# Efficient attention and a channel MLP on one core: the first batches' work put in another order, and batch 0's x transposed by TensorE

## The chip, the cores and the metric

The kernel runs on one core of a Trainium2 chip. The metric is the device time in microseconds (us), and what counts is the median of the runs. Engines are named as in the profile: PE (TensorE, matmuls), DVE (VectorE), ACT (ScalarE), POOL (GpSimd), and SP (SyncE, whose queue issues nearly all DMAs).

## The reference

q, k and v have 8 batches, 8 heads, 576 tokens and 64 channels. In each head, q's exponentials are divided by their sum over the channels, k's by their sum over the tokens, and the output is `q' (k'^T v)`. The heads of one token side by side are x (8 x 576 x 512), which goes through a two-layer channel MLP with a residual:

```python
q_s = np.exp(q_s); q_s = q_s / (np.sum(q_s, axis=-1, keepdims=True) + 1e-09)
k_s = np.exp(k_s); k_s = k_s / (np.sum(k_s, axis=2, keepdims=True) + 1e-09)
kv = np.einsum('bhsd,bhse->bhde', k_s, v)
attn = np.einsum('bhsd,bhde->bhse', q_s, kv)
x = attn.transpose(0, 2, 1, 3).reshape(B, S, H * D)
xn = (x - mu) / np.sqrt(var + 1e-06) * g_ln          # mu, var over the 512 channels
out = x + np.maximum(xn @ w_ch1, 0.0) @ w_ch2         # 512 -> 2048 -> 512
```

## The kernel before

**Chunks.** Tokens are worked in 9 chunks of 512: the first 512 of each of the 8 batches, and a ninth (`xT8`, `x8`) of the 64 that are left over in each. All weights stay in SBUF in fp16.

**Attention of a batch** (`attn`, L309). q, k and v come in halves of four heads (hf 0 and 1) into staging buffers `stg` of fp32. `queries` takes exponentials on ACT (L326) and the sums, reciprocals and products on DVE (L328 to L332). `keys` and `values` are one ACT instruction each (L353 and L359, 128x1152). `eq` is transposed to `eqT`, for batch 0 by PE and copies out of PSUM (`pe_t`, L341: L349 on DVE, L350 on ACT), for all others by a DMA transpose from SP (L337). `kv` (L362) multiplies k by v; the column of ones in `vb` gives the sum of k, whose reciprocal (L378) scales `kve` (L381 on ACT, L385 on DVE). `xT` (L390) makes x transposed, `xsT`, copied out by L409 or L411; `xT_last` (L414) does the 64 tokens left over.

**Tokens** (`tokens`, L480). `xsT` is turned into x by a DMA transpose (L487, on SP), then come the statistics on DVE (L490, L491) and the inverse deviation `st` on ACT by Ln and Exp (L492, L494).

**MLP of a chunk.** The first layer, `mm1` (L521), is 16 blocks of four 128x512 matmuls (L538), each taken out of PSUM with a ReLU to `hT` (ACT L501, or DVE L503 in part of batch 0). The mean is not subtracted from x: w1 is centred once, in four column blocks (`centre_w1`, L275: a sum by a matmul with ones, L282, a copy `nm` on ACT, L284, and subtractions on DVE, L288), after it was cast and scaled by g (`load_w1`, L256: L269 on ACT, L272 on DVE). For batch 0, `mm1_open` (L509) starts blocks 0 to 3 with the first heads alone. The second layer of batch 0 is `mm2` (L672): 64 plain matmuls in 16 groups of four (L681), evicted by L694 once the statistics are there. From batch 1 on it is `mm2_split` (L591), seven products of half size with sums of `hT` (`S`, L554) and of w2 (`T`, `w2_sums`, L560); partial results are read out between products by `add_x` into `cp` and by `final` into `ot` (all L628).

**PSUM.** Eight banks: four `pg` for the MLP, four `pa` for the attention and for w1's sums; batch 1's first four mm1 blocks also use `pa`. `zeros` (L705) are matmuls of zeros that fill PE's waits in the head.

**Order.** Each step is added to a `Plan` (L22) with an engine, an estimated duration, what it reads and writes, and a class `cls`; `after` adds an order without data. `Plan.order` simulates the engines and a DMA queue, and at each moment takes the ready step of the lowest class. The instructions are then written out in that order, and each engine executes its own strictly in that order. So a class or an estimate changes nothing but places in the engines' queues. Fills are as many as the planner's gap holds (L119). In the head, `first_w1` (L717) puts block 0's centring and `mm1_open` between the transposes and the k and v of batch 0's second heads.

Of the kernel before, what the change touches and what calls it, by code (L numbers as in the profile page):

```python
# [21 lines left out]
class Plan:  # L22
# [33 lines left out]
    def order(self):  # L56
# [11 lines left out]
        queue = 1.2  # L68
# [5 lines left out]
        while done < n:  # L74
            best = None
            for eng, lst in pend.items():
                if not lst:
                    continue
                f = free.get(eng, 0.0)
                t0 = max(f, min(ready[i] for i in lst))  # L80
                c = min((i for i in lst if ready[i] <= t0 + 1e-9), key=lambda i: T[i][4])
                if best is None or t0 < best[0]:
                    best = (t0, c, eng)
            t0, i, eng = best
            pend[eng].remove(i)
            _, dur, fn, deps, _, land, mb = T[i][:7]
            start[i] = t0
            issued = end = t0 + dur
            if mb or land:
                queue = max(queue, t0 + min(dur, 0.6)) + mb / 0.385  # L90
                issued = max(end, queue - (9.0 if dur < 2.0 else 0.8))
                end = max(queue, issued) + land
            free[eng] = issued
            for u in users[i]:
                hop = (self.HOP if T[u][0] != eng or mb or land else 0.0) + T[u][9]
                ready[u] = max(ready[u], issued if i in T[u][7] else end + hop)
                left[u] -= 1
                if left[u] == 0:
                    pend.setdefault(T[u][0], []).append(u)
            seq.append(i)  # L100
            done += 1
# [9 lines left out]
    def emit(self):  # L111
        seq = self.order()
        open_, at = None, 0.0
        for i in seq:
            if self.tasks[i][0] == "PE":
# [3 lines left out]
                n = int((self.start[i] - at - 0.1) / self.FILL)  # L119
# [20 lines left out]
def kernel(  # L140
# [46 lines left out]
    hold = sb([P, 1], FP32, "hold")  # L187
# [50 lines left out]
    def load(dst, src, w, mb):  # L238
        gate[1] = plan.add("SP", 0.55, lambda: nc.sync.dma_start(dst, src), w=w, mb=mb, land=2.0,
                           after=tuple(gate[0]) + ((gate[1],) if gate[1] is not None else ()))  # L240
# [15 lines left out]
    def load_w1(blk):  # L256
        after = state["kve"] if blk == 1 else state["ev"][1] if blk == 2 else ()
        cls = 0.5 if blk else 0
        for kp in range(2):
            s = nxt("stg", NST)  # L260
            load(stg[s][:, :1024].rearrange("p (a n) -> p a n", a=2),
                 w1_src[:, 2 * kp : 2 * kp + 2, blk * 512 : blk * 512 + 512], sk(s), 0.524 if blk else 0.65)
            for a in range(2):
                ko = 2 * kp + a
                dst = w1_sb[:, ko, blk * 512 : blk * 512 + 512]
                src = stg[s][:, a * 512 : a * 512 + 512]
                gk = g_sb[:, ko : ko + 1]
                if ko % 2:
# [6 lines left out]
    def centre_w1(blk):  # L275

        gi = nxt("pa", 4)
        cs = slice(blk * 512, blk * 512 + 512)
        wk = [("w1", blk, ko) for ko in range(KO1)]
        def f():  # L280
            for ko in range(KO1):
                nc.tensor.matmul(pa[gi], ones, w1_sb[:, ko, cs], start=(ko == 0), stop=(ko == KO1 - 1))  # L282
        plan.add("PE", 0.216 * KO1, f, r=wk + ["ones"], w=[("pa", gi)], cls=0)
        plan.add("ACT", act_t(512), lambda: nc.scalar.copy(nm, pa[gi]), r=[("pa", gi)], w=["nm"], cls=0)  # L284
        for k0, k1, m0, m1 in ([(0, 2, 0, 4), (2, 4, 0, 4)] if blk == 0 else [(0, 4, 0, 1), (0, 4, 1, 4)]):
            n = (m1 - m0) * P
            c0 = blk * 512 + m0 * P
            plan.add("DVE", dve_t((k1 - k0) * n, 2), lambda k0=k0, k1=k1, c0=c0, n=n, m0=m0: nc.vector.tensor_tensor(  # L288
                w1_sb[:, k0:k1, c0 : c0 + n], w1_sb[:, k0:k1, c0 : c0 + n],
                nm[:, m0 * P : m0 * P + n].unsqueeze(1).to_broadcast([P, k1 - k0, n]), op=ALU.subtract),  # L290
                r=["nm"] + wk, w=[("w1c", 4 * blk + m, k) for m in range(m0, m1) for k in range(k0 // 2, k1 // 2)], cls=0)

# [10 lines left out]
    ident_b = sb([P, P], BF16, "ident_b")  # L303
    plan.add("POOL", 1.5, lambda: make_identity(nc, ident_b), w=["ident"])
    XK = lambda u: [("xsT", u, j, g) for j in range(J) for g in range(G)]
# [3 lines left out]
    def attn(b, kind, between=None, exps=(), sums_=(), kvs=()):  # L309
# [31 lines left out]
        def pe_t(hf):  # L341
# [5 lines left out]
            plan.add("PE", 0.7, f, r=[("eq", u, hf), "ident"], w=[("pa", t) for t in tb], cls=0)  # L347
            dst = eqT[u][:, JT * hf : JT * hf + 8]
            plan.add("DVE", dve_t(1024, 2), lambda: nc.vector.tensor_copy(dst, v16[0]), r=[("pa", tb[0])], w=[("eqT", u, hf)], cls=0)  # L349
# [7 lines left out]
        def values(hf, s):  # L357
            vd, va = vb[u][:, hf].rearrange("p j s d -> p s j d")[:, :, :, :D], sv(s)
            plan.add("ACT", act_t(QW), lambda: nc.scalar.copy(vd, va), r=sk(s), w=[("vb", u, hf, i) for i in range(2)],  # L359
                     cls=cls, slack=late, after=tuple(exps) + (tuple(state["ev"][-1][-1:]) if steady else ()))  # L360

        def kv(hs):  # L362
# [9 lines left out]
            ids = []  # L372
            plan.add("PE", 0.1 + 0.42 * len(hs), f, r=[("ek", u, h) for h in hs] + [("vb", u, h, i) for h in hs for i in range(2)],
                     w=[("pa", a) for x in ab for a in x], cls=0, slack=SLACK if steady else 0.2, after=kvs)
            for n, h in enumerate(hs):
                for e in range(2):
                    a, g = ab[n][e], 2 * h + e
                    plan.add("DVE", 0.17, lambda a=a, g=g: nc.vector.reciprocal(rz[:, g : g + 1], pa[a][:, D : D + 1]),  # L378
                             r=[("pa", a)], w=[("rz", g)], cls=0.35 if steady else 0)
                    if e and not steady:  # L380
# [3 lines left out]
                    else:  # L384
                        ids.append(plan.add("DVE", 0.28, lambda a=a, g=g: nc.vector.tensor_scalar_mul(  # L385
                            kve[u][:, g, :], in0=pa[a][:, :D], scalar1=rz[:, g : g + 1]),
                            r=[("pa", a), ("rz", g)], w=[("kve", u, g)], cls=0.35 if steady else 0))
            return ids

        def xT(hs, after=()):  # L390
# [12 lines left out]
            for n, h in enumerate(hs):  # L403
                for i in range(2):
# [3 lines left out]
                    if kind == "first" and i == 1:  # L408
# [23 lines left out]
        if kind == "first":  # L432
            lq, lk, lv = [load_half(b, t, 0, x) for t, x in ((q, 0), (k, 0), (v, 0.25))]
# [5 lines left out]
            pe_t(0)  # L439
# [3 lines left out]
            pe_t(1)  # L443
            between()
            lk, lv = [load_half(b, t, 1) for t in (k, v)]
# [3 lines left out]
            state["kve"] = kv([1])  # L449
            xT([1])  # L450
# [13 lines left out]
        else:  # L464
            gate[1] = dma_t()
            state["eqT"] = gate[1], tokens(0, 0.7, (gate[1],))
# [13 lines left out]
    def tokens(c, cls=1, after=(), stats=()):  # L480
# [4 lines left out]
        else:  # L485
            src, r = xT8, [("xT8", b, i) for b in range(B) for i in range(2)]
        i = plan.add("SP", 2.2, lambda: nc.sync.dma_start_transpose(x.rearrange("p j (k c) -> p (j k) c", k=KO1), src.rearrange("p n t -> p (n t)")),  # L487
                 r=r, w=[(xk, j) for j in range(J)], mb=0.9, land=0.6, after=after)
        for j in range(J):
            plan.add("DVE", dve_t(512), lambda j=j: nc.vector.bn_stats(bst[:, j, :], x[:, j, :]), r=[(xk, j)], w=[("bst", j)], cls=cls, slack=2.0 if c else 0.5, after=stats)  # L490
# [4 lines left out]
                 r=[(stk, "v", j) for j in range(J)], w=[(stk, "r", j) for j in range(J)], cls=0)  # L495
# [64 lines left out]
    def w2_sums(k0, n, after):  # L560
# [6 lines left out]
        def tt(i, a, b, r):  # L567
            eng, e = ("POOL", nc.gpsimd) if i == 2 else ("DVE", nc.vector)
            plan.add(eng, 1.2 if i == 2 else dve_t(256 * n, 2), lambda: e.tensor_tensor(T[i][:, ks], a, b, op=ALU.subtract),  # L569
                     r=r + (["hold"] if i == 2 else []), w=tk(i), cls=2, after=after if i == 2 else ())  # L570
# [101 lines left out]
    def mm2(c):  # L672
# [4 lines left out]
        for k0 in range(0, KO2, 4):  # L677
            for j in range(J):
# [5 lines left out]
                if j == 0:  # L684
                    ids.append(i)
                if (k0, j) in steps:
                    second_x(steps.index((k0, j)), (i,))
        plan.fill(ids[0], ids[-1], zeros(pg[gis[0]], False))
        evs = []
        for hf in range(2):  # L690
            o = nxt("ot", NOT)
            for i in range(2):
                j = 2 * hf + i
                ev = plan.add("DVE", dve_t(512), lambda o=o, i=i, j=j: nc.vector.scalar_tensor_tensor(  # L694
# [3 lines left out]
                evs.append(ev)  # L698
            store(c, o, hf)
        return evs[:1]  # L700
# [16 lines left out]
    def first_w1():  # L717
        centre_w1(0)
# [21 lines left out]
    for b in range(B):  # L740
        if b:
            state["tok"] = tokens(b, 0.7, stats=state["stats"])
        if b == B - 1:
            tokens(8, 0.7, stats=state["stats"])
        ids = mm1(b, b > 0, () if b else opened)
# [5 lines left out]
        before = (ids[-1], state["rstd"])  # L751
        if b == 0:
            evs = mm2(b)
            plan.add("POOL", 0.2, lambda: nc.gpsimd.tensor_copy(hold, ot[0][:, 0, :1]), r=[("ot", 0, 0)], w=["hold"])
            for k0 in range(0, HK, 2):
                w2_sums(k0, 2, evs)
        else:
            mm2_split(b)
    mm1(8, True)
# [37 lines left out]
```

The softmax here doesn't subtract the row's maximum and nothing guards it: scores larger than these inputs give would overflow.

## Time and profile before

| | |
|---|---|
| median of 9 runs | 280.9 us (280.61 to 281.1) |
| the profiled execution | 281.06 us |
| its span | 279.3 us |
| PE busy | 270.1 us, 97% |
| DVE busy | 199.2 us, 71% |
| ACT busy | 168.2 us, 60% |
| POOL busy | 5.9 us, 2% |
| TensorE's granted clock | 0.998 |
| DMA | 55.35 MB, about 387 GB/s from 10 to 40 us |

The span is what the profiler covers of the execution; the rest of its time lies outside. In the profile's timeline a row is start, length, engine, line, operation, `out<-in` and, in brackets, the engine's idle time before the row and what ended it. In the chain of waits a row is start, length and what the time went to, followed back from the last instruction. A matmul of 512 columns is listed with 0.38 us, but in a stream they start 0.216 us apart.

### The profile page before, as it was taken

Reading aid. Unit: us, or ns where it says so; the run is one execution under the profiler, and the core shown is the slowest. Engines: PE = TensorE matmul, PEld = TensorE weight load, DVE = VectorE, ACT = ScalarE, POOL = GpSimd, SP = SyncE. Lnnn points to the kernel's source line nnn. Section 1 sums busy time; section 2 is a strip of 40 time slices with the busy share of each in tenths; the row PEclk is TensorE's granted clock in tenths of the full one; section 3 lists DMA queues with packets and bytes.
Section 4 is the critical chain, followed back from the end, with each engine's and each line's share of the span. In section 5 each row is a group of like instructions: output and inputs, shape, how many; then the busy total and the mean of one; then the engine's idle time right before and its main releaser. Section 6 shows DMA issues by size and latency. Waiting matters only on the chain.

```text
span 279.3 us, 5657 instructions
## 1 busy us (share of the span) xinstructions
PE 270.1 (97%) x2327; PEld 164.5 (59%) x2327; DVE 199.2 (71%) x406; ACT 168.2 (60%) x273; POOL 5.9 (2%) x15
## 2 busy tenths in 40 slices
PE   8989999989799999999999999999999999999994
PEld 3434444435674478447844784478447844874583
DVE  2867897499859967976599569865995773641572
ACT  4768985499478595568566946685665077016500
POOL 1000000060000000000000000000000000000000
PEclk9999999999999999999999999999999999999999
DMA  7999998999987894579858985697544350023004
GB/s 257 354 386 387 387 389 196 270 341 236 318 266 153 207 392 73 150 153 387 131 151 109 396 166 150 137 392 143 153 84 78 75 153 0 0 51 101 0 2 151
DMA packets 57953, 55.35 MB, mean 198 GB/s; under 512 B 36676, under 2 KB 37192, under 8 KB 57928
## 3 DMA queue, kind: packets, MB, share of 16 engines
q1 hardware_dynamic: 57776, 54.86, 68.1%
q8 instruction: 18, 0.29, 0.4%
q10 hardware_dynamic: 152, 0.13, 0.1%
q14 instruction: 7, 0.06, 0.1%
HBM read 36.70 MB, written 9.44 MB: 165 GB/s over the span
## 4 chain that ended last, share of the span: by engine, by line
PE 78%; DVE 13%; DMA 6%; ACT 1%; issue 1%; SPq 0%
PE pg L538 38%; PE pg L618 32%; DMA stg<-in_moe_w_ch_dram 4%; PE pg L705 3%; DVE zq L328 2%; DVE eq L332 2%; DMA x<-xsT 2%; DVE S L554 2%; DVE bst L490 2%; PE pa L370 1%; PE pa L618 1%; PE pa L398 1%; DVE ot L694 1%; DVE T L569 1%; PE pa L282 1%
## 5 line engine op out<-in xcount | busy, mean ns | idle before, releaser
L501 ACT ACTIVATE hT<-pg 128x512 f16<-128x512 f32 x134 | 78.9, 600 | 67.2 <-PE pg L538 66.6
L538 PE MATMUL pg<-xsT,w_sb 128*128 128x512 f16 x488 | 108.2, 379 | 1.0 <-ACT hT L501 0.4
L538 PEld LDWEIGHTS <-w_sb 128*128 128x128 f16 x568 | 54.9, 98 | 65.9 <-issue 1.3
L618 PEld LDWEIGHTS <-S 128*128 128x128 f16 x512 | 49.7, 98 | 7.6 <-issue 1.5
L618 PE MATMUL pg<-T,S 128*128 128x256 f16 x368 | 42.2, 273 | 1.5 <-DVE cp L628 1.5
L618 PEld LDWEIGHTS <-hT 128*128 128x128 f16 x384 | 37.0, 98 | 8.2 <-issue 3.0
L554 DVE TENSOR_TENSOR S<-hT 128x1024 f16<-128x1024 f16 x32 | 21.8, 685 | 23.7 <-ACT hT L501 23.7
L628 DVE SCALAR_TENSOR_TENSOR cp<-pg,st,x 128x256 f32<-128x256 f32 x46 | 20.2, 478 | 13.3 <-PE pg L618 12.6
L618 PE MATMUL pg<-w_sb,hT 128*128 128x256 f16 x248 | 29.4, 273 | 0.0
L490 DVE BATCH_NORM_STATS2 bst<-x 128x6 f32<-128x512 f16 x36 | 24.1, 671 | 7.1 <-DMA x<-xsT 7.1
L628 DVE SCALAR_TENSOR_TENSOR ot<-pg,st,cp 128x256 f32<-128x256 f32 x47 | 20.5, 477 | 11.6 <-PE pg L618 11.5
L332 DVE TENSOR_TENSOR eq<-eq,rzq 128x1152 bf16<-128x1152 bf16 x16 | 22.7, 1418 | 0.5
L359 ACT CAST vb<-stg 128x1152 f16<-128x1152 f32 x16 | 18.7, 1168 | 5.5 <-DMA stg<-in_v_dram 5.4
L328 DVE TENSOR_REDUCE zq<-eq 128x18 f32<-128x1152 bf16 x16 | 21.5, 1345 | 0.3 <-ACT eq L326 0.3
L326 ACT ACTIVATE eq<-stg 128x1152 bf16<-128x1152 f32 x16 | 18.8, 1177 | 2.9 <-DMA stg<-in_q_dram 2.7
L353 ACT ACTIVATE ek<-stg 128x1152 bf16<-128x1152 f32 x16 | 18.7, 1166 | 2.6 <-DMA stg<-in_k_dram 2.6
L411 ACT CAST xsT<-pa 128x512 f16<-128x512 f32 x30 | 15.5, 598 | 2.4 <-PE pa L398 2.4
L705 PE MATMUL pg<-zero 128*128 128x512 f16 x52 | 14.3, 422 | 1.2 <-DVE zero L224 1.2
L618 PE MATMUL pg<-w_sb,S 128*128 128x256 f16 x128 | 15.3, 273 | 0.0
L618 PE MATMUL pg<-T,hT 128*128 128x256 f16 x120 | 14.4, 272 | 0.4 <-DVE ot L628 0.4
L681 PE MATMUL pg<-w_sb,hT 128*128 128x512 f16 x64 | 14.7, 380 | 0.0
L538 PE MATMUL pg<-xT,w_sb 128*128 128x512 f16 x64 | 14.0, 379 | 0.0
(64 smaller groups left out, 164.6 us busy)
## 6 DMA issues: line engine op xcount, KB each, us to landing
stg<-in_q_dram SPq DMA_DIRECT2D x16, 576.0 KB, 5.6
stg<-in_k_dram SPq DMA_DIRECT2D x16, 576.0 KB, 7.3
stg<-in_v_dram SPq DMA_DIRECT2D x16, 576.0 KB, 8.0
out_dram<-ot SPq DMA_DIRECT2D x33, 256.0 KB, 3.6
stg<-in_moe_w_ch_dram SPq DMA_DIRECT2D x16, 512.0 KB, 10.1
out_dram<-ot SPq DMA_DIRECT2D x1, 512.0 KB, 2.8
x<-xsT SPq DMA_TRANSPOSE x8, 6.7
out_dram<-ot SPq DMA_DIRECT2D x1, 128.0 KB, 2.7
```

Source lines behind the costliest of these rows:

```text
L326: plan.add("ACT", act_t(QW), lambda: nc.scalar.activation(e.rearrange("p j (s d) -> p s j d", s=2), sv(s), AF.Exp), r=sk(s), w=[("eq", u, ...
L328: plan.add("DVE", dve_t(QW), lambda: nc.vector.reduce_sum(zq[:, hf], eh, axis=AX.X), r=[("eq", u, hf)], w=[("zq", hf)], cls=qcls, after=sums_)
L332: plan.add("DVE", dve_t(QW), lambda: nc.vector.tensor_tensor(eh, eh, rzq[:, hf].to_broadcast([P, 2 * JT, D]), op=ALU.mult), r=[("rzq", hf) ...
L353: plan.add("ACT", act_t(QW), lambda: nc.scalar.activation(ek[u][:, hf].rearrange("p j (s d) -> p s j d", s=2), sv(s), AF.Exp), r=sk(s), w= ...
L359: plan.add("ACT", act_t(QW), lambda: nc.scalar.copy(vd, va), r=sk(s), w=[("vb", u, hf, i) for i in range(2)], cls=cls, slack=late, after=t ...
L490: plan.add("DVE", dve_t(512), lambda j=j: nc.vector.bn_stats(bst[:, j, :], x[:, j, :]), r=[(xk, j)], w=[("bst", j)], cls=cls, slack=2.0 if ...
L501: nc.scalar.activation(hT[:, m, :], bank, AF.Relu)
L538: nc.tensor.matmul(bank[gi], w1_sb[:, ko, m * P : m * P + P], xt[:, ko], start=(ko == 0), stop=(ko == KO1 - 1))
L554: plan.add("DVE", dve_t(256 * n, 2), lambda: nc.vector.tensor_tensor(S[i][:, ks], a, b, op=op), r=r, w=sk(i), cls=0.3 if k0 else 0.45)
L618: nc.tensor.matmul(g[i][0], fa(k, i), fb(k), start=(first and k == 0 and (i == 0 or g[0][1] != g[1][1])), stop=(last and k == HK - 1), ski ...
L628: nc.vector.scalar_tensor_tensor(dst[:, i, :], in0=g[i][0], scalar=sti[:, 4, 2 * t0 + i : 2 * t0 + i + 1], in1=src[:, i, :], op0=ALU.mult, ...
L705: nc.tensor.matmul(bank_, zero[:, :P], zero, start=start, stop=start, skip_group_check=True)
```

## The change

All of it lies in what happens up to batch 2; batch 0 changes most.

1. The v cast of batch 0's second heads is two instructions: channel group 0 on DVE, 1 on ACT.
2. `centre_w1(0)` uses the bank `pg[opened[2]]`; its second subtraction is held back behind the kv of the second heads, and the copies of the second transposes (`pe_t_evac`) behind the first subtraction. The `nm` copies get a lower class.
3. w1's casts are split otherwise over ACT and DVE (`on_act`), and those of block 2 on ACT need only follow the `nm` copy before them.
4. Batch 0's x is made by 16 PE transposes into two `pa` banks and two DVE copies, inside `mm2`, with no DMA transpose.
5. `w2_sums` is all on DVE; the POOL instructions and `hold` are gone.
6. In `kv` the two reciprocals come ahead of the two products; which engine scales `kve` and in which class is set by batch. `xT` of batch 0 has three ACT copies and one DVE copy.
7. The planner's constants: DMA queue start, rate, landing time, the margin taken off a fill, the class of batch 1's statistics.

```diff
-        queue = 1.2
+        queue = 2.4
...
-                n = int((self.start[i] - at - 0.1) / self.FILL)
+                n = int((self.start[i] - at - 0.45) / self.FILL)
...
-    hold = sb([P, 1], FP32, "hold")
...
-        gate[1] = plan.add("SP", 0.55, lambda: nc.sync.dma_start(dst, src), w=w, mb=mb, land=2.0,
+        gate[1] = plan.add("SP", 0.55, lambda: nc.sync.dma_start(dst, src), w=w, mb=mb, land=0.65,
...
+        on_act = ((1,), (0, 1, 3), (1,), (1, 3))[blk]
...
+                after = state["kve"] if blk == 1 and (kp or ko not in on_act) else ()
+                if blk == 2:
+                    after = (state["nm"],) if ko in on_act else state["ev"][1]
...
-                if ko % 2:
+                if ko in on_act:
...
-        gi = nxt("pa", 4)
+        if blk:
+            gi = nxt("pa", 4)
+            bank, bk = pa[gi], ("pa", gi)
+        else:
+            bank, bk = pg[opened[2]], ("pg", opened[2])
...
-        plan.add("ACT", act_t(512), lambda: nc.scalar.copy(nm, pa[gi]), r=[("pa", gi)], w=["nm"], cls=0)
+        state["nm"] = plan.add("ACT", act_t(512), lambda: nc.scalar.copy(nm, bank), r=[bk], w=["nm"], cls=-0.5)
...
+        if blk == 0:
+            state["sub"] = sub(0, 2, 0, 4)
+            return lambda: sub(2, 4, 0, 4)
+        sub(0, 4, 0, 1)
+        sub(0, 4, 1, 4)
...
+    ident_h = sb([P, P], FP16, "ident_h")
+    plan.add("POOL", 1.5, lambda: make_identity(nc, ident_h), w=["ident_h"])
...
+            if kind == "first" and hf == 1:
+                plan.add("DVE", dve_t(QW // 2, 2), lambda: nc.vector.tensor_copy(vd[:, 0], va[:, 0]), r=sk(s), w=[("vb", u, hf, 0)], cls=cls)
+                plan.add("ACT", act_t(QW // 2), lambda: nc.scalar.copy(vd[:, 1], va[:, 1]), r=sk(s), w=[("vb", u, hf, 1)], cls=cls)
+                return
...
+            kcls = 0 if not steady else 0.35 if b > 2 else -0.6
...
-                    if e and not steady:
+                for e in range(2):
+                    a, g = ab[n][e], 2 * h + e
+                    if e and (b == 1 or b == 2 or h and not b):
...
-                    if kind == "first" and i == 1:
+                    if kind == "first" and i == 1 and h == 1:
...
-            lq, lk, lv = [load_half(b, t, 0, x) for t, x in ((q, 0), (k, 0), (v, 0.25))]
+            lq, lk, lv = [load_half(b, t, 0, x) for t, x in ((q, 0), (k, 0), (v, 0))]
...
-            pe_t(0)
+            pe_t_evac(0, *pe_t(0))
...
-            pe_t(1)
+            t1 = pe_t(1)
             between()
+            pe_t_evac(1, *t1, (state["sub"],))
...
             state["kve"] = kv([1])
+            state["sub2"]()
             xT([1])
...
-            state["eqT"] = gate[1], tokens(0, 0.7, (gate[1],))
+            state["eqT"] = (gate[1],)
...
+        i = None
+        for hf in range(2) if c == 0 else ():
+            t = nxt("pa", 4)
+            v = pa[t].bitcast(FP16)
+            def f(hf=hf, v=v):
+                for n in range(8):
+                    nc.tensor.transpose(v[:, n * P : n * P + P], src[:, 8 * hf + n, :], ident_h)
+            plan.add("PE", 0.52, f, r=r + ["ident_h"], w=[("pa", t)], cls=0, after=after)
+            plan.add("DVE", dve_t(1024, 2), lambda hf=hf, v=v: nc.vector.tensor_copy(
+                x[:, 2 * hf : 2 * hf + 2, :], v.rearrange("p (j n) -> p j n", j=2)), r=[("pa", t)], w=[(xk, 2 * hf), (xk, 2 * hf + 1)], cls=cls)
+        if c:
+            i = plan.add("SP", 2.2, lambda: nc.sync.dma_start_transpose(x.rearrange("p j (k c) -> p (j k) c", k=KO1), src.rearrange("p n t -> p (n t)")),
+                     r=r, w=[(xk, j) for j in range(J)], mb=0.9, land=0.6, after=after)
...
-            eng, e = ("POOL", nc.gpsimd) if i == 2 else ("DVE", nc.vector)
...
+            plan.add("DVE", dve_t(256 * n, 2), lambda: nc.vector.tensor_tensor(T[i][:, ks], a, b, op=ALU.subtract),
+                     r=r, w=tk(i), cls=2)
...
+                if (k0, j) == (4, 2):
+                    tokens(0, 0.7, (i,))
...
-            state["tok"] = tokens(b, 0.7, stats=state["stats"])
+            state["tok"] = tokens(b, 0.7 if b > 1 else 0.35, stats=state["stats"])
...
-            plan.add("POOL", 0.2, lambda: nc.gpsimd.tensor_copy(hold, ot[0][:, 0, :1]), r=[("ot", 0, 0)], w=["hold"])
```

## The prediction

> **What bounds the kernel now.** I read the 40 slices first (is TensorE full everywhere?), then the chain of waits in order of time (where does it leave TensorE?), then TensorE's own timeline of the head. The slices:
>
> ```profile
> PE   8989999989799999999999999999999999999994
> ```
>
> Each is 7 us; the holes are in the first eleven. The chain's later part is TensorE alone:
>
> ```profile
> 102.94 8.84 PE pg L618 x80
> 111.78 9.50 PE pg L538 x44
> 121.28 0.76 PE pa L370 x72
> 122.04 4.42 PE pg L538 x20
> ```
>
> Columns: start, length, what. Each begins where the last ends, so from about 83.8 us a batch costs its matmuls, and no step of the change takes one away there. The head is different:
>
> ```profile
> 24.34 0.43 DVE w_sb L288
> ...
> 45.95 5.95 DMA x<-xsT
> 51.91 0.02 issue
> 51.93 0.70 DVE bst L490
> ...
> 55.83 2.73 DVE ot L694 x4
> ...
> 74.43 0.89 DVE cp L628 x2
> 75.31 0.04 issue
> 75.36 5.41 PE pg L618 x48
> ```
>
> The path runs from a weight that is centred late, over the DMA transpose of x0, its statistics and batch 0's eviction, to batch 1's first `cp`. What TensorE loses there, in brackets (idle before, and who ended it):
>
> ```profile
> 18.55 0.48 PE L370 MATMUL pa<-vb,ek 64*64 64x65 f16 x36 [0.92 <-ACT vb L359]
> 24.82 1.90 PE L538 MATMUL pg<-xsT,w_sb 128*128 128x512 f16 x8 [0.30 <-DVE w_sb L288]
> 56.63 3.61 PE L538 MATMUL pg<-xsT,w_sb 128*128 128x512 f16 x16 [0.29 <-DVE ot L694]
> 60.67 7.07 PE L538 MATMUL pg<-xsT,w_sb 128*128 128x512 f16 x32 [0.43 <-ACT hT L501]
> 75.36 1.91 PE L618 MATMUL pg<-T,S 128*128 128x256 f16 x16 [1.50 <-DVE cp L628]
> 81.72 1.91 PE L618 MATMUL pg<-T,hT 128*128 128x256 f16 x16 [0.41 <-DVE ot L628]
> ```
>
> By starts the loss is a little larger, since listed ends overlap: batch 1's 64 mm1 matmuls take 52.72 to 67.57 = 14.85, the same 64 at 223.22 take 13.81, so 1.04 is lost; batch 1's mm2 takes 67.57 to 83.82 = 16.25 against 13.18 (98.60 to 111.78) + 0.76 for the kv matmuls inside it = 13.94, so 2.31 is lost. One 4-matmul block is 0.865.
>
> **v cast on two engines.** v of the second heads lands at 17.34 (ACT starts its 1.17 cast then, kv follows at 18.55). Half on ACT: 0.60 for a 128x512 cast, so 0.65 for 576. Half on DVE: 0.68 for a 1024 fp32 cast (L298), so about 0.5; at the slow rate of L409 (0.69 for 512) 0.75. I take 0.65: kv at 18.05, 0.5 earlier (0.4 to 0.5). On DVE the first centring subtract (0.63), the eqT copy (0.6), two reciprocals and a product (0.5) now queue behind the v half, so behind 17.34. The subtract ends at 18.45, kv at 18.5: no new wait. `mm1_open` runs 18.55 to 20.3, xT follows at 20.4 (ACT's two weight casts of 0.65 and kve end at 20.15).
>
> **Centring ahead of copies.** Before, block 1's subtract stood on DVE behind a cast of block 3, landing 23.92. Now the last cast ahead of it is block 2's, landing 22.56 (the second of DVE's two at 21.97 + 1.10 - 0.48): cast to 23.05, subtract of the first quarter 0.43, 23.5. TensorE: xT 20.4, centring at 20.9 once ACT and DVE have cast block 1's last pair, 0.86, xT_last 0.18, 8 matmuls 1.73: 23.75. So block 4 starts at 23.75 instead of 24.82, **1.07 earlier**, the v gain and the two 0.22 fills counted. The casts that changed engine fit between evictions; I find blocks 5 to 15 back to back, mm2 of batch 0 at 35.87. Block 0's centring sum goes to bank pg2, copied out by 16.1, opened by mm1 at 19.4: no wait.
>
> **x0 by TensorE.** 16 transposes. L346 does 9 in 0.63 on the chain, 0.07 each: 1.12. The Trainium skill ("TensorE: Matmul & The Clock Gate", Part 4) gives about 275 ns for one in a kernel's context[...]; that would be 4.4 and would turn the whole change to a loss of about 1.1. I take the row: same shape, two-byte data, back to back, and nothing waits on one alone. In before the DMA transpose left SP 1.84 and landed 5.95 after its issue, and DVE sat 3.81 idle for it. Timeline now: mm2 group 11 ends 45.4; kv needs v casts (44.82 and 46.35; the loads of k and v land 1.5 apart, the load queue is the limit, so these stay); kv, one group, kv: 47.2; transposes to 48.4; four groups and three small products: mm1 of batch 1 at **52.65**, against 52.72. The head's 1.07 is eaten by the transposes; the gain has to come from behind.
> DVE: kv's reciprocals and products to 47.85, two copies out of PSUM at 0.61 (L349) to 49.1, four statistics pairs at 0.79 to 52.3, Ln and Exp 0.55 on ACT: 52.85. Eviction of batch 0 52.9 to 55.6 instead of 55.83 to 58.56. Bank pg0 is wanted at 56.1: the stalls of 0.29 and 0.43 go, **1.04** by starts.
>
> **T2 from POOL to DVE, hold removed.** Four at 0.385 = 1.54 on DVE, at 42 to 48, where before had 0.32 + 0.69 + 3.81 idle; costs nothing while w2's cast for k0=8 still ends (41.4) before 42.8. POOL makes one more identity (0.2 + 0.29) ahead of `ident_g`, which TensorE wants at 5.7: hidden. The POOL group goes, and with it the one `eq` product that took 2.35 beside it where the others take 1.36.
>
> **x1's statistics earlier.** SP's queue without x0: eqT of batch 1, two q loads, x1's transpose at 51.85 (ACT's last xsT copy), landing about 57.2 (4.3 to 6.0 for these). DVE then: eviction 55.6, sum 56.9, reciprocal 57.2, x1's four pairs 60.5, eq product 61.9, sum, reciprocal, product 64.8, S sums; `cp` of 11*11 at 69.6. TensorE, leaving mm1 at 66.5, wants it at 70.0: the 1.50 goes. With no wait at all mm2 would end at 66.5 + 13.94 = 80.45: 3.37 won.
>
> **What is late next.** ACT's order. Two kve scalings of batch 2 move to ACT and stand behind batch 3's two q exponentials. Those wait for loads that SP issues after eqT of batch 2 (its DVE product ends 64.8, SP takes 3.2: 68.05). In before the issues at 68.88 and 69.4 landed at 74.74 and 76.22; so 73.9 and 75.4 to 75.5. ACT: 75.5 + 1.16 + 0.31 = 77.0. TensorE arrives at xT at 76.1: **0.9 lost**. Then two k exponentials (landing 78.4 at the latest) to 79.55, four xsT copies 2.05: 81.6, and TensorE is at 81.35: 0.3 lost. Batch 2 starts at 81.65 instead of 83.82: **-2.15**. After that the orders on PE, DVE and ACT differ only in which bank or which reciprocal comes first; ten microseconds lie between xsT and its use: 0.
> Planner constants, the 0.45 margin for fills: no instruction's price, only order and fewer fills (52 to 33 zero matmuls), all in waits: 0, but see the clock.
>
> **Sum.** The profiled execution took 281.06, 1.76 of it outside its span of 279.3; 281.06 - 2.15 = 278.9. It stood 0.16 above the median of 280.9, so 278.75; I say **278.8**.
>
> **Rivals.**
> (1) *No wait on ACT's q.* If the loads land by 74 (eqT moves a little faster) nothing is late: 280.9 - 3.4 = 277.5. For it: nothing else is due. Against: landing hangs on 4.6 to 6.5 us of DMA transpose ahead. 20%.
> (2) *TensorE's clock falls.* Fills go from 27 to 22 ahead of the first transposes and to none from about 14 us on. I count idle of 1.2, 0.35, 0.65 and 1.5 between 11 and 18.1; the longest in before was 0.92. The skill, same page ("HAM oscillation" and its table of rules), warns of idle gaps above some 3 us; a gap of 1.5 is inside that. But it also says that transposes do not count as work, and then 15.3 to 18.1 is one gap of 2.8. Price from the trace: cold loads stand 0.427 apart up to 4.6 us, warm 0.216; 3.4 us cold lose 1.7. As kv of batch 1 slips with it, so does all behind: 278.8 + 1.7 = 280.5, no change. I take the gap rule; before's 0.92 and its granted clock of 0.998 say no more. 13%.
> (3) *Slower: eqT of batch 1 runs into v.* Its `eq` product ends at 40.8 instead of 42.66, so SP issues this transpose while k, v0 and v1 are still under way; in before only v0 and v1 were. If transfers share instead of queueing, v1 lands up to one transpose (4.6) late, at 49.8; kv of batch 1 then starts at 51.0, not 46.75, and copies, statistics, eviction, x1 and q slide by 4.2: 283. It decides from v1 landing after 47.7 (2.15 late). Against: in before k0, k1, v0, v1 came at an even 1.5 although the transpose was issued between. Small delays give 279 to 280. 11%.
> (4) *The change is not what it says*, since a planner sets the order: no; built, DVE, ACT, PE and SP stand in the order used above.
>
> **Numbers.** Likeliest case 56%, its own range 278.1 to 279.6. With (1), 20%; (2), 13%; (3), 11%. The range 277.2 to 280.7 takes in the no-wait bound and the cold clock, and leaves out (3). A difference under 0.2% (0.56 us) cannot be told from none: below 280.3 counts as faster (56 + 20 and a little of the rest, 0.77), to 281.5 as the same (0.12), above as slower (0.11).
>
> **What would show it.** Right: kv of batch 0's second heads about 18.05; mm1 block 4 at 23.7; 16 transposes in about 1.2; mm1 of batch 1 near 52.6 with no gap; `cp` not waited for; an idle piece near 76 before L398's counterpart, ended by ACT's kve behind q; batch 2 at 81.6. Wrong: matmuls 0.427 apart after 18; v1's cast after 47.7; x1 landing after 58; any gap inside a batch past 84, which I put at nothing and which would count six times.

## The result, and the profile after

The changed kernel takes **277.72 us** (median of 10 runs, 277.37 to 278.22), the one before 280.79 in the runs beside it (31 runs, 280.41 to 281.66): ratio 0.989, 95% interval 0.9882 to 0.9898. The profiled execution took 277.66, its span 275.9, at a granted clock of 1.000. PE is busy for 268.3 us, DVE 199.0, ACT 168.1, POOL 1.7 (5.9 before).

The chain of waits of the changed kernel (start, length, what), up to batch 2:

```profile
9.04 11.97 DMA stg<-in_moe_w_ch_dram
...
21.04 0.72 ACT w_sb L271
21.76 1.47 ACT hT L538 x3
...
23.27 1.91 PE pg L575 x8
...
52.46 3.45 PE pa L575 x16
55.91 10.36 PE pg L575 x48
66.27 5.24 PE pg L654 x48
```

Before, the chain ran from batch 0 over the DMA transpose of x0, its statistics, batch 0's eviction and `cp`. Now it is the load of w1 up to 21.04, then ACT, and from 23.27 on nothing but TensorE to the last instructions. At 23.27 two things had just ended: the three ReLUs on ACT that the chain names (23.23), and the first piece of block 1's subtraction on DVE (22.79 + 0.42 = 23.21). It was the subtraction that block 4 waited for: in a run below block 4 starts at 22.46, while the same three ReLUs end at 23.33. TensorE's own timeline (start, length, engine, line, operation, and in brackets the idle time before it):

```profile
16.40 0.48 PE L391 MATMUL pa<-vb,ek 64*64 64x65 f16 x36
...
23.27 1.91 PE L575 MATMUL pg<-xsT,w_sb 128*128 128x512 f16 x8 [1.03 <-ACT hT L538]
...
35.37 9.66 PE L717 MATMUL pg<-w_sb,hT 128*128 128x512 f16 x44
...
46.75 1.07 PE L519 MATMUL pa<-ident_h,xsT 128*128 128x128 f16 x16
47.66 1.03 PE L717 MATMUL pg<-w_sb,hT 128*128 128x512 f16 x4
...
52.30 3.62 PE L575 MATMUL pa<-xsT,w_sb 128*128 128x512 f16 x16
55.75 10.52 PE L575 MATMUL pg<-xsT,w_sb 128*128 128x512 f16 x48
66.11 3.66 PE L654 MATMUL pg<-w_sb,hT 128*128 128x256 f16 x32
69.60 1.91 PE L654 MATMUL pg<-T,S 128*128 128x256 f16 x16
...
75.80 0.63 PE L422 MATMUL pa<-eqT,kve 64*64 64x512 bf16 x8
```

From 16.40 to the end the timeline lists a single wait on TensorE, the one at block 4 (23.27). The 64 matmuls of batch 1's mm1 take 66.11 - 52.30 = 13.81, what they take undisturbed. Where the time came from, by starts on TensorE:

| stage begins | before | predicted | after |
|---|---|---|---|
| mm1 block 4, batch 0 | 24.82 | 23.75 | 23.27 |
| mm2, batch 0 | 36.92 | 35.87 | 35.37 |
| mm1, batch 1 | 52.72 | 52.65 | 52.30 |
| mm2, batch 1 | 67.57 | 66.5 | 66.11 |
| mm1, batch 2 | 83.75 | 81.65 | 80.21 |
| mm1 of the ninth chunk | 249.10 | | 245.80 |

So 1.55 is won by mm2 of batch 0. At mm1 of batch 1 0.42 of it is left: the transposes take 0.91, and small pieces the rest. Then 1.04 comes from mm1's stalls, since batch 0's eviction starts at 52.50 instead of 55.83, and 2.08 from mm2's: 3.54 in all.

```profile
52.50 2.73 DVE L731 SCALAR_TENSOR_TENSOR ot<-pg,st,x 128x512 f32<-128x512 f32 x4 [0.29 <-ACT st L531]
```

Batch 2 gives back 0.24 (by the chain it takes 28.20, before 27.96: 0.13 more in its first 44 matmuls, 0.11 more in the kv matmuls behind them), and 3.30 reaches the end in this pair of executions. The medians differ by 3.07.

At the place where the prediction saw the next wait, SP's timeline (the DMA transpose of batch 2's `eq`, then batch 3's q) and ACT's:

```profile
64.29 3.18 SPq L351 DMA_TRANSPOSE eqT<-eq  x1
67.51 1.10 SPq L238 DMA_DIRECT2D stg<-in_q_dram  x2
```

```profile
71.92 1.16 ACT L340 ACTIVATE eq<-stg 128x1152 bf16<-128x1152 f32 x1 [1.84 <-DMA stg<-in_q_dram]
72.99 0.30 ACT L405 ACTIVATE kve<-pa,rz 128x64 f16<-128x64 f32 x1
73.45 1.16 ACT L340 ACTIVATE eq<-stg 128x1152 bf16<-128x1152 f32 x1 [0.16 <-DMA stg<-in_q_dram]
74.52 0.30 ACT L405 ACTIVATE kve<-pa,rz 128x64 f16<-128x64 f32 x1
```

Both `kve` scalings do stand behind batch 3's q exponentials, but the second ends at 74.82, ahead of xT at 75.80.

### The profile page after: what moved, and what is told of

The parts are those of the page before. It is cut to its first block, busy times and chain, and to the rows that moved or that the text cites. A ratio compares the mean times of both kernels' runs of the same rounds, so it can differ in the third digit from the quotient of the medians.

```text
span 275.9 us, 5670 instructions
## 1 busy us (share of the span) xinstructions
PE 268.3 (97%) x2324; PEld 163.9 (59%) x2324; DVE 199.0 (72%) x412; ACT 168.1 (61%) x274; POOL 1.7 (1%) x12
## 4 chain that ended last, share of the span: by engine, by line
PE 90%; DMA 7%; ACT 1%; SPq 0%; DVE 0%; issue 0%
PE pg L575 43%; PE pg L654 35%; PE pg L717 5%; DMA stg<-in_moe_w_ch_dram 4%; DMA stg<-in_v_dram 2%; PE pa L391 2%; PE pa L422 1%; PE pa L654 1%; PE pa L575 1%; PE pa L288 1%; ACT hT L538 1%; PE pa L445 0%; ACT vb L380 0%; PE pa L519 0%; SPq L238 0%; ACT w_sb L271 0%
## 5 line engine op out<-in xcount | busy, mean ns | idle before, releaser
L346 DVE TENSOR_TENSOR eq<-eq,rzq 128x1152 bf16<-128x1152 bf16 x16 | 21.6, 1353 | 0.3
L380 ACT CAST vb<-stg 128x1152 f16<-128x1152 f32 x15 | 17.6, 1172 | 2.9 <-DMA stg<-in_v_dram 2.9
L740 PE MATMUL pg<-zero 128*128 128x512 f16 x33 | 10.7, 486 | 1.2 <-DVE zero L223 1.2
```

The source lines that it names most:

```text
L346: plan.add("DVE", dve_t(QW), lambda: nc.vector.tensor_tensor(eh, eh, rzq[:, hf].to_broadcast([P, 2 * JT, D]), op=ALU.mult), r=[("rzq", hf) ...
```

## The experiments

Times are compared with runs of the kernel before on the same chip. "Alone" means one part of the change put into the kernel before; "undone" means one part taken out of the changed kernel. Where a run is set against the changed kernel, two medians are subtracted that were not taken side by side; worked out from the ratios instead, the differences are 0.65 for x0, 0.84 for the statistics, 0.67 for the zeros and 1.7 for the first subtraction. Two of the undone parts (x0 and the statistics) and x0 alone went through the planner, which also moved other steps (in the first two, batch 2's `kve` scalings on ACT), so their times are those of the part with its new order.

**The kernel before, once more.** No edit.

> The kernel before once more, for its trace. In the first trace v of batch 0's second heads landed at 17.3 us, after the change at 15.6 or earlier, although SP issued it at 4.6 in both. If landing is set by the order of casts and issues, v lands again at 17.0 to 17.6 here and batch 3's q some 9.1 us after the issue of batch 2's eqT transpose. If it scatters from execution to execution, v lands anywhere from 15 to 17.5, with the time near 280.8 all the same, because block 4 of mm1 still waits for w1's third block (24.8).

281.6 in one run, span 279.8. The landing scatters. v of the second heads was there by 15.85 in this execution (17.34 in the first trace), kv ran at 17.68, and still block 4 waited 0.97 and started at 24.62. DVE's timeline says why:

```profile
22.39 0.49 DVE L272 TENSOR_SCALAR w_sb<-stg,g_sb 128x512 f16<-128x512 f32 x1 [0.82 <-DMA stg<-in_moe_w_ch_dram]
23.74 0.49 DVE L272 TENSOR_SCALAR w_sb<-stg,g_sb 128x512 f16<-128x512 f32 x1 [0.87 <-DMA stg<-in_moe_w_ch_dram]
24.15 1.28 DVE L288 TENSOR_TENSOR w_sb<-w_sb,cp 128x512 f16<-128x512 f16 x2
```

Two casts that wait for their load stand ahead of the subtraction (L288) that block 4 needs. In the same view of the changed kernel the last such cast ahead of it is the one for the load before, and the subtraction comes 1.36 earlier:

```profile
21.04 0.49 DVE L274 TENSOR_SCALAR w_sb<-stg,g_sb 128x512 f16<-128x512 f32 x1 [0.94 <-DMA stg<-in_moe_w_ch_dram]
22.39 0.48 DVE L274 TENSOR_SCALAR w_sb<-stg,g_sb 128x512 f16<-128x512 f32 x1 [0.87 <-DMA stg<-in_moe_w_ch_dram]
22.79 1.29 DVE L294 TENSOR_TENSOR w_sb<-w_sb,cp 128x512 f16<-128x512 f16 x2
```

So the head's gain is the place of this subtraction in DVE's queue, counted in loads of w1 that land about 1.35 apart. It does not hang on one execution: with the head of before (four profiles: the two of this kernel, x0 alone, the statistics alone) block 4 starts at 24.37 to 24.82 and mm2 of batch 0 at 36.48 to 36.92; with the changed head (the changed kernel, x0 undone, the statistics undone) at 23.00 to 23.40 and 35.10 to 35.51. The old place of the subtraction was not put back alone.

**v cast whole on ACT, undone through the planner.**

```diff
-            if kind == "first" and hf == 1:
+            if False:
```

> The kernel after, with the second heads' v cast whole by ACT. Theory (block 4 of mm1 waits for the landing of w1's third block at 22.4, so that nothing won before counts): 277.7 within 0.3. Rival (the prediction's own count, v gives 0.4 to 0.5 of the head's gain): 278.1 to 278.3.

282.23 (6 runs), ratio 1.0054 (1.0037 to 1.0071): slower than before. It is no test of the cast. Block 4 started at 23.39, 0.12 later; but the planner, told of a longer cast, set everything behind in another order: kv of batch 1's second heads at 50.52 (46.34 in the changed kernel), mm1 of batch 1 at 54.85 and of batch 2 at 85.76, with eight waits on the way. One estimate in the plan was worth 4.5 us; neither expectation had that. The next run keeps the order.

**v cast whole on ACT, every place kept.** The DVE step stays in the plan and does nothing; ACT casts both groups.

```diff
-                plan.add("DVE", dve_t(QW // 2, 2), lambda: nc.vector.tensor_copy(vd[:, 0], va[:, 0]), r=sk(s), w=[("vb", u, hf, 0)], cls=cls)
-                plan.add("ACT", act_t(QW // 2), lambda: nc.scalar.copy(vd[:, 1], va[:, 1]), r=sk(s), w=[("vb", u, hf, 1)], cls=cls)
+                plan.add("DVE", dve_t(QW // 2, 2), lambda: None, r=sk(s), w=[("vb", u, hf, 0)], cls=cls)
+                plan.add("ACT", act_t(QW // 2), lambda: nc.scalar.copy(vd, va), r=sk(s), w=[("vb", u, hf, 1)], cls=cls)
```

> The changed kernel with one thing undone: v of batch 0's second heads is cast whole on ACT (1.17 us instead of 0.65 beside DVE), and every instruction's place in every queue is kept. My prediction gave the cast 0.4 to 0.5 us at kv. Theory (T): what limits the head is the landing of w1 behind v, so block 4 of mm1 stays within 0.15 of 23.27 although kv of the second heads comes 0.4 later, and the time is 277.7 to 278.0. Rival (R): kv's 0.5 goes through to block 4 and from there to the end, 278.2 to 278.3.

277.71 (5 runs), ratio 0.9886 (0.9867 to 0.9905): no different from the changed kernel. kv waited 0.56 for ACT, but block 4 still hung on the subtraction (22.62 here), and mm2 of batch 0 started at 35.19. The split cast is worth nothing here.

**x0 by DMA transpose, undone.**

```diff
-            state["eqT"] = (gate[1],)
+            state["eqT"] = gate[1], tokens(0, 0.7, (gate[1],))
...
-        for hf in range(2) if c == 0 else ():
+        for hf in ():
...
-        if c:
+        if True:
...
-                if (k0, j) == (4, 2):
-                    tokens(0, 0.7, (i,))
```

> The kernel after, with batch 0's x made by a DMA transpose behind eqT of batch 1 again, and no PE transposes. Theory (their 0.9 us on TensorE buys an eviction 2 to 3 us earlier): x0 lands near 51, eviction from 54.8, TensorE waits for pg banks again, eqT of batch 2 leaves about 2 us later and with it q and k of batch 3: 280.0 us (279.2 to 280.8). Rival (the DMA transpose was hidden, the transposes only cost): 276.8, 0.9 below the kernel after.

278.29 (4 runs), ratio 0.9913 (0.9898 to 0.9928): 0.57 more than the changed kernel, far less than expected, and barely clear of noise (the two intervals meet at 0.9898). TensorE, without the transposes, begins mm1 of batch 1 at 51.43 and meets no wait in it, because x0's statistics start at 49.85 (51.93 before). Of these 2.08, 0.80 come from the issue of the transpose (45.15 on SP, 45.95 before) and 1.28 from its landing, 4.7 after the issue instead of 5.95; why it landed sooner, no run shows. Against the changed kernel they are 1.23 late, and so is the rest of DVE's queue behind them: batch 0's eviction at 53.74 instead of 52.50, eqT of batch 2 on SP at 65.58 instead of 64.29, and q of batch 3 lands later. ACT's timeline, then TensorE's:

```profile
73.23 1.16 ACT L340 ACTIVATE eq<-stg 128x1152 bf16<-128x1152 f32 x1 [3.72 <-DMA stg<-in_q_dram]
74.30 0.50 ACT L405 ACTIVATE kve<-pa,rz 128x64 f16<-128x64 f32 x2
```

```profile
74.29 0.98 PE L422 MATMUL pa<-eqT,kve 64*64 64x512 bf16 x8
...
78.43 0.25 PE L445 MATMUL pa<-eqT,kve 64*64 64x64 bf16 x6 [0.27 <-ACT xsT L435]
```

xT stands at 74.29 and is drawn out to 0.98 (0.63 in the changed kernel): it waits for `kve`, which ACT runs from 74.30, behind q. That is the wait of the prediction, in another kernel.

**x0 by PE transposes, alone.** The core of the edit to the kernel before, with the identity, the two DVE copies and `tokens(0)` inside `mm2` as in the change:

```diff
+            plan.add("PE", 0.52, f, r=r + ["ident_h"], w=[("pa", t)], cls=0, after=after)
...
+                if (k0, j) == (4, 2):
+                    tokens(0, 0.7, (i,))
```

> The kernel before with one part of the change alone: batch 0's x by 16 PE transposes and two DVE copies in place of the DMA transpose. Theory (T): the three stalls behind batch 0's eviction (0.29, 0.43) and the 1.50 at cp get smaller, since eviction comes some 3 us earlier and SP's queue is one transpose shorter, while the transposes cost 0.9 on TensorE: net gain 1.5 to 2.0, 278.8 to 279.3. Rival (R): without the other parts x1's statistics stay late behind batch 0's eviction or the DVE sums, the 1.50 stays, and the 0.9 of the transposes is only just repaid by the mm1 stalls: 280.4 to 280.9.

279.86 (4 runs), ratio 0.9959 (0.9945 to 0.9974), between the two expectations. All four stalls between 52 and 84 are gone, the 1.50 at `cp` among them, though x1's statistics are still late here (the last pair at 67.79). So mm1 of batch 2 begins at 81.29, 2.46 earlier than before. At the end 1.88 of that is left (the last DVE instruction at 273.50 against 275.38); in the profiled run the last store then took 3.2 us to land, where the others took 2.2 or 2.3, so that the span is only 1.0 shorter. The median is 1.24 below that of before; whether the store was as late in the other runs, no profile shows. T2 stays on POOL here (53.70 to 58.19), and DVE's first `eq` product, which runs beside it, is slow again:

```profile
57.07 2.35 DVE L334 TENSOR_TENSOR eq<-eq,rzq 128x1152 bf16<-128x1152 bf16 x1
...
61.01 1.36 DVE L334 TENSOR_TENSOR eq<-eq,rzq 128x1152 bf16<-128x1152 bf16 x1
```

**Batch 1's statistics late, undone.**

```diff
-            state["tok"] = tokens(b, 0.7 if b > 1 else 0.35, stats=state["stats"])
+            state["tok"] = tokens(b, 0.7, stats=state["stats"])
```

> The kernel after, with batch 1's statistics put back into class 0.7, so that they stand behind the q products and the first S sums on DVE. Theory (the gain is made behind 52 us, by x1's statistics coming before the sums): the last statistics pair ends near 70, cp near 71.4, TensorE waits 1.5 to 2 us for it, 279.5 us (279.0 to 279.9). Rival (batch 0's earlier eviction alone pays; x1's statistics would be in time anywhere): 277.5 to 278.0.

278.53 (4 runs), ratio 0.992 (0.9905 to 0.9935): 0.81 more than the changed kernel, between the two expectations. x1's last pair comes at 69.20 on DVE (59.06 in the changed kernel), and a wait for `cp` is back on TensorE, two thirds of the one before. DVE's timeline, then TensorE's:

```profile
73.90 1.66 DVE L664 SCALAR_TENSOR_TENSOR cp<-pg,st,x 128x256 f32<-128x256 f32 x4 [0.75 <-PE pg L654]
```

```profile
74.83 1.91 PE L654 MATMUL pg<-T,S 128*128 128x256 f16 x16 [0.97 <-DVE cp L664]
```

This `cp` had itself waited 0.75 for one of TensorE's products, not for the statistics (the first `cp` ran at 70.70). So the wait came with the order that the planner made for late statistics; that the statistics alone cause it is not shown.

**Batch 1's statistics early, alone.** The same line, put into the kernel before.

> The kernel before with one part alone: the class of batch 1's statistics (x1's four pairs come ahead of the sums of eq on DVE). Theory (T): x0's eviction still ends at 58.6 there, so x1's pairs end about 62 and delay eq's product and SP's transpose of eqT behind it; the 1.50 at cp shrinks, but q and k of batch 3 land some 3 us later: net 279.6 to 280.3. Rival (R): the 1.50 goes whole and nothing is late, 279.3 or less; or the delay at q takes it all, 280.6 and more.

280.89 (10 runs), ratio 0.9996 (0.9982 to 1.0009): nothing. x1's pairs now run from 59.48 to 62.7 on DVE, but batch 0's eviction still ends at 58.3, and the second `eq` product comes 1.8 us later behind them (65.90 instead of 64.09), with the sums S after that. TensorE's waits have moved, not gone:

```profile
71.83 1.91 PE L618 MATMUL pg<-T,S 128*128 128x256 f16 x16 [0.40 <-DVE cp L628]
...
81.04 0.60 PE L618 MATMUL pg<-T,hT 128*128 128x256 f16 x4 [0.96 <-DVE ot L628]
```

T2 ran on POOL from 56.53 to 61.03 in this run; the first `eq` product came behind it, at 62.95, and took 1.36. So it is the time beside POOL that made this product slow, 2.35, in the runs where they met. The edit pays only once x0 comes early. Parts of one change are not to be added up.

**No zeros after 8 us.**

```diff
-                n = int((self.start[i] - at - 0.45) / self.FILL)
+                n = int((self.start[i] - at - 0.45) / self.FILL) if self.start[i] < 8.0 else 0
```

> The changed kernel without any matmul of zeros after 8 us (the ones before stay). Theory (T): the clock does not fall, since idle pieces of about 1 us left it at 1.0 in the changed kernel; the matmuls from 17 to 24 us start 0.216 apart, and the time is 277.7 within 0.3. Rival (R): the fills from 8 to 15 us hold the clock up; without them matmuls after 15 us start 0.427 apart for some 3 us, block 4 of mm1 comes 1 to 1.7 later, and the time is 278.7 to 279.5.

17 of the 33 zero matmuls go. 278.82 (4 runs), ratio 0.9914 (0.9894 to 0.9935): 1.1 more by the medians, where the intervals still touch; the trace shows that the rival was right. Busy time in three stretches (core time, then PE with its instructions, PEld, DVE, ACT and POOL, the granted clock, the share of DMA and GB/s):

```profile
8.00:11.00 3.00, 1.18 (x46) 0.99 (x46) 2.12 (x6) 2.49 (x3) 0.00 (x0) 1.00 1.02 327
11.50:21.00 9.50, 8.20 (x64) 3.11 (x64) 7.17 (x15) 6.00 (x11) 0.00 (x0) 0.50 1.05 392
22.00:26.00 4.00, 4.00 (x26) 1.73 (x25) 3.85 (x9) 3.53 (x7) 0.00 (x0) 1.00 1.05 388
```

With TensorE busy for 1.18 of the 3 us before 11, the clock is granted at half from 11.4 to 21.6, and mm2 of batch 0 begins at 36.37 instead of 35.37. In the changed kernel the same 3 us are full with zeros (3.00), and the clock stays at 1.00.

**The first subtraction ahead of block 2's casts.**

```diff
-                    after = (state["nm"],) if ko in on_act else state["ev"][1]
+                    after = (state["nm"],) if ko in on_act else (state["sub1"],)
...
-        sub(0, 4, 0, 1)
+        state["sub1"] = sub(0, 4, 0, 1)
```

> The changed kernel with one dependence moved: the subtraction of block 1's first quarter of w1 is put on DVE ahead of block 2's casts there, which waited for w1 to land (0.94 and 0.87 us of DVE idle) and held the subtraction back. Theory (T): block 4 of mm1 then starts when the centring sum is copied out, at 22.1 to 22.4 instead of 23.27; about 0.9 of it reaches batch 1, and the time is 276.7 to 277.0. Rival (R): blocks 8 to 11 now wait for their later casts, or kv of batch 1 for v (cast at 45.08, kv not before 46.3), and the gain is lost by mm1 of batch 1: 277.5 to 277.8.

279.63 (4 runs), ratio 0.995 (0.9936 to 0.9964): slower than the changed kernel by 1.9, which neither expectation had. Block 4 came without a wait at 22.46. But the planner now put a w2 cast ahead of block 2's subtraction, and that cast waits for its load. DVE, then TensorE:

```profile
29.07 0.69 DVE L310 CAST w_sb<-stg 128x1024 f16<-128x1024 f32 x1 [1.09 <-DMA stg<-in_moe_w_ch_dram]
29.68 0.42 DVE L605 TENSOR_TENSOR T<-w_sb 128x512 f16<-128x512 f16 x1
30.01 1.28 DVE L294 TENSOR_TENSOR w_sb<-w_sb,cp 128x512 f16<-128x512 f16 x2
```

```profile
25.92 1.89 PE L288 MATMUL pa<-w_sb,ones 128*128 128x512 f16 x8
30.49 7.09 PE L575 MATMUL pg<-xsT,w_sb 128*128 128x512 f16 x32 [2.67 <-DVE w_sb L294]
```

It is the same fault one block later, and dearer.

**Places moved by hand.** In these the planner's order stands, and a list moves single steps within their engine's queue (each to just behind another; only the list is shown):

```diff
...
+    (('cast2', 0), ('sub1', 1)),
+    (('cast2', 1), ('cast2', 0)),
+    (('cast2', 2), ('cast2', 1)),
+    (('w2DVE', 0), ('sub2', 1)),
+    (('T', 0), ('w2DVE', 0)),
+    (('w2DVE', 1), ('sub3', 1)),
+    (('T', 1), ('w2DVE', 1)),
+    (('mm2', 11), ('mm2', 10)),
+    (('mm2', 12), ('kv1', 0)),
+    (('mm2', 13), ('x0T', 1)),
+    (('xT1', 1), ('xT1', 0)),
...
```

> The changed kernel in its own order but for a few steps moved by hand: on DVE the subtractions of blocks 1, 2 and 3 of w1 stand ahead of the casts that wait for the next weights (three casts of w1 block 2, two of w2 with a difference each); on TensorE one group of mm2 more stands ahead of batch 1's kv, and xT of both halves together, since that kv cannot come before v has landed (46.3). Theory (T): block 4 of mm1 starts at 22.1 to 22.3 instead of 23.27, no later block waits more than 0.3, mm2 of batch 0 starts at 34.5, mm1 of batch 1 at 51.4 instead of 52.3; then the exponentials of batch 3's k, which wait for their load (76.5 and 77.9), hold back the xsT copies of batch 2 behind them on ACT, and 0.5 to 0.8 of the 0.9 is lost there: 277.2 to 277.6. Rival (R): the wait moves on in the head, as it did in the previous kernel with this aim, and mm2 starts later than 35.2: 277.7 to 278.5.

277.71 (6 runs), ratio 0.9887 (0.9867 to 0.9906): not told apart from the changed kernel. Block 4 waits no more, but a later one waits 0.62 for a ReLU on DVE, and mm2 of batch 0 begins at 35.07. The exponentials of batch 3's k, which stand ahead of batch 2's xsT copies on ACT, cost no more than in the changed kernel: batch 2 at 79.71, its first 44 matmuls in 9.80. In the second kernel they (`ek3`) are moved behind these copies (`xsT2`):

> The kernel head_moved with the two exponentials of batch 3's k put behind batch 2's four xsT copies on ACT. Theory (T): nothing behind waits for them (batch 3's kv is some 20 us away), so mm1 of batch 2 starts at 79.3 instead of 80.2 without being drawn out, and the whole 0.9 reaches the end: 276.8 to 277.0, faster than both kernels. Rival (R): q of batch 3 and its exponentials, ahead of two kve scalings, become the wait at xT (TensorE arrives at 74.9, the last scaling ends at 74.8 in the changed kernel), or the staging buffers come free later and the next loads with them: 277.3 to 278.

278.12 (6 runs), ratio 0.9911 (0.9889 to 0.9933): no gain either. The 44 matmuls now take 9.67, so the k exponentials had cost 0.13. TensorE has the same 0.62, and on ACT the second `kve` scaling is now the last before xT (75.31), behind q:

```profile
32.49 2.75 PE L613 MATMUL pg<-xsT,w_sb 128*128 128x512 f16 x12 [0.62 <-DVE hT L578]
```

```profile
73.71 1.16 ACT L378 ACTIVATE eq<-stg 128x1152 bf16<-128x1152 f32 x1
74.78 0.30 ACT L443 ACTIVATE kve<-pa,rz 128x64 f16<-128x64 f32 x1
```

The third takes both waits away (the second w2 cast behind block 9's ReLU; batch 3's q exponentials behind the `kve` scalings):

```diff
-    (('w2DVE', 1), ('sub3', 1)),
+    (('w2DVE', 1), ('hTD', 3)),
...
+    (('q3', 0), ('kve2', 1)),
+    (('q3', 1), ('q3', 0)),
```

> The kernel head_copies with its two new waits taken away: on DVE the ReLU of block 9 stands ahead of the second w2 cast and its difference (TensorE waited 0.62 for it), and on ACT batch 2's two kve scalings stand ahead of the exponentials of batch 3's q (xT waited for the second one). Theory (T): mm2 of batch 0 starts at 34.5, kv of batch 1's second heads again at 46.3 (v's landing), mm1 of batch 1 at 51.2, xT of batch 2 at 74.3 to 74.6 and batch 2 at 78.5 to 78.9 instead of 80.2: 276.1 to 276.7. Rival (R): something that the two waits covered comes last instead (the sums S and cp on DVE, which the statistics of x1 hold back until 64), and batch 2 starts at 79.5 or later: 277.2 to 277.8.

**276.89** (5 runs, 276.47 to 278.06), ratio 0.9853 (0.9825 to 0.988): below both kernels, if narrowly below the changed one, and between the two expectations. TensorE:

```profile
34.16 10.52 PE L757 MATMUL pg<-w_sb,hT 128*128 128x512 f16 x48
...
51.01 3.62 PE L615 MATMUL pa<-xsT,w_sb 128*128 128x512 f16 x16
...
78.86 9.67 PE L615 MATMUL pg<-xsT,w_sb 128*128 128x512 f16 x44
...
137.89 7.07 PE L615 MATMUL pg<-xsT,w_sb 128*128 128x512 f16 x32 [0.42 <-DVE ot L704]
```

1.2 earlier at mm2 and 1.35 at batch 2; the ninth chunk's share of that is smaller, since later batches have small stalls like the last row's, and the last DVE instruction ends 0.76 earlier than in the changed kernel.

## Why the prediction was right or wrong

The direction was right, and the time foretold was too long by 1.1 us: its likeliest case did not come about, and its rival (1) did. Two pieces of luck have a part in it: v landed late in the one trace that the head's gain was counted from, and q landed early in the changed kernel. Step by step:

- **v cast, 0.4 to 0.5.** Wrong as a gain. kv of the second heads ran at 16.40, not 18.05, since v landed by 15.64 here; the 17.34 of the trace was one execution's landing. With the early landing, too, block 4 hung on w1 (the second run of before), and the cast whole in the same place costs nothing (277.71).
- **Centring ahead of copies, 1.07.** Right in its mechanism, mis-sized: 1.55 against the first trace, 1.35 against the second. It put the subtraction behind the cast of block 2, at 22.56 + 0.48, and it came at 22.79. But it had TensorE arrive last, at 23.75 (its terms add up to 23.67); with v landed early TensorE was there at 22.24, and the subtraction set the time.
- **x0 by TensorE, 1.12.** 0.91 (46.75 to 47.66), 0.057 each. The row of L346 was the right choice; with 275 ns each from the Trainium skill ("TensorE: Matmul & The Clock Gate", Part 4) it would have been 4.4, which no run here shows.
- **Eviction earlier, 1.04 of mm1's stalls.** Right: 52.50 to 55.2 for 52.9 to 55.6, and 13.81 for the 64 matmuls. But the PE path is not needed for it: with the DMA transpose put back there is no mm1 stall either, as it leaves 0.80 earlier in the new order and landed sooner.
- **T2 to DVE, nothing.** Its `eq` products take 1.32 and 1.36, and the 2.35 came back where T2 stayed on POOL and met one of them. What the move is worth alone was not tried.
- **x1's statistics, the 1.50.** The wait is gone, and with the statistics late again a wait of 0.97 stands near its place. But the gain is not theirs alone: x0 by PE transposes took the 1.50 away in the kernel before with the statistics left late. (The 2.31 lost in mm2 took its end from the chain and its start from TensorE's timeline; on the timeline alone it is 2.24.) That they help only together with an early x0 (nothing alone) the prediction did not say, though its own timeline has it: x1's pairs stand behind the eviction.
- **What is late next, 0.9 and 0.3 lost.** This step failed. The order on ACT was read rightly, and the wait exists (x0 by DMA transpose shows it). The term of the sum that was mis-sized is q's landing: 73.9 and 75.4 foretold, 71.92 and about 73.4 found. The product ahead of eqT ended at 64.05 (64.8), q left SP at 67.51 (68.05), and it landed 4.41 after its issue, where I had taken 5.86 from the one trace. In the nine other profiles that show it, it was 4.3 to 6.0, so the 5.86 was a long one but no stray: with it, from 67.51, the second scaling would have ended at about 76.3 (an estimate: 67.51 + 5.86 + 1.5 to the second load + 1.16 + 0.3), and xT would have waited 0.5. The 0.3 for the k exponentials was 0.13.
- **The rest of the kernel, nothing.** 0.24 was given back in batch 2, 0.13 of it through the k exponentials.

**Rival (1)** is what happened, with 277.5 for 277.72; the 0.24 of batch 2 is about the difference. **Rival (2)** did not come about, with a clock of 1.000, but its mechanism is real: without fills after 8 us the clock halves, and the cost was 1.00 at mm2 of batch 0 where I had put 1.7. **Rival (3)** is out: v of batch 1 was cast at 45.08.

## What to carry to other kernels

An instruction whose inputs are there can stand on its engine behind another that waits for a load; its place was worth up to a load's spacing here (1.35 us). Look for such pairs first, and after moving one look for the same fault a block later. Take landing times from several executions, and price the next wait by their spread, not by one trace. Parts of a change that take waits off one path are worth different sums alone and together (statistics early: nothing alone, 0.81 in company; x0 by TensorE: 1.24 alone, 0.57 in company), and with a planner a test that alters an estimate tests the plan, not the part; keep the order fixed.

## What was not expected of the hardware

- The clock fell to half at 11.4, though TensorE had been at work again since 9.11. The Trainium skill ("TensorE: Matmul & The Clock Gate", the table of rules at its end) asks for no idle gap above some 3 us; without fills the longest one was 2.51 (6.60 to 9.11), then 0.71 and 0.50. If the nine transposes at 9.11 are left out, as rival (2) does, the longest is 3.11 (6.60 to 9.71). Whether it is such a gap that counts or the busy share (1.18 of 3 us), this run does not show. The clock came back at 21.6, with TensorE busy without a gap from 15.42 on.
- The landing of one and the same load differs between two executions of the kernel before by 1.5 us or more: v of batch 0's second heads, issued at 4.6, came at 17.34 in one and was there by 15.85 in the other.
- A DMA transpose of `eq` holds SP for 2.4 to 5.0 us in these runs, and loads behind it leave later by as much.
